# The first four tiles of x: loaded as rows and turned on TensorE in place of a transposing load, with new instruction orders

## The chip, the cores and the metric

The kernel runs on one core of one Trainium2 chip. The metric is the device time of one execution in microseconds (us); the number given for a kernel is the median of several runs. One execution of each kernel is also recorded by the hardware profiler. Its trace gives each instruction's start and length, counted from the start of the recorded span.

## The reference

The input x has 2048 rows of 448 columns, in bfloat16. The result mixes an attention block A and a token-mixing block B by a gate per row:

```python
x = A_x
g = _sigmoid((x * gate_w).sum(-1, keepdims=True))
a = _A_ref(x, A_wq, A_wk, A_wv, A_wo, A_beta)
b = _B_ref(x, B_w1, B_b1, B_w2, B_b2)
return g * a + (1 - g) * b
```

A projects x to q, k and v (16 heads of 28 columns) and works in four segments of 512 rows. In each segment it takes causal softmax attention within the segment, and adds, by a second gate per head, what a running memory of the earlier segments gives: the memory sums phi(k) v, with phi(t) = t + 1 above zero and exp(t) below. The heads are joined and multiplied by wo. B normalizes each row of x, multiplies over the rows with w1 (2048 by 1792), adds a bias, applies GELU, multiplies with w2 back to 2048 rows and adds a bias.

## The kernel before, in words

All work is written as small named operations, each with the data that it reads and writes. The class Sched turns them into instruction streams for five engines: TensorE (PE), ScalarE (ACT), VectorE (DVE), GpSimd (POOL) and SyncE (SP), of which SP issues most DMAs and ACT the first few. The order on each engine is not computed: the table ORDER spells it out, name by name, and some operations may stand on either of two engines, as the table says. Waits follow from the data. Each engine runs its list strictly in order, so an instruction that waits holds everything behind it.

x is used in two layouts. As rows (tile xh, 16 tiles of 128 rows) it feeds the normalization and B's first product. Turned (tile xT, the 448 columns cut into four overlapping chunks of 128 on the partitions, the rows along the free dimension) it feeds the projections. xT is filled in four groups of 512 rows, each by two transposing DMAs from device memory: dtx0_0 and dtx0_1 for the first group, dtx1, dtx2 and dtx3 for the later ones (transpose_x, line 546). The row tiles are loaded four at a time (load_x, line 532).

The program starts so. SP issues the two transposing loads of group 0, then parts of wk and wq, then the transposing loads of group 1, then the four row loads. ACT issues three parts of wv, the gate vector, the fourth part of wv, the last part of wk and two biases; then comes the one load of its activation table, which stands ahead of its first ACTIVATE. TensorE runs nine passes over a constant of ones (warm_up, line 660, operation warm), turns the gate vector (gtr), and then projects v for row tiles 0 to 3. A v tile is summed over four chunks of xT. Chunk 0 alone is the operation pra, chunk 1 prb, and the last two are one whole pass (prt) and a half of the array's rows in a step that two tiles share (lot0, lot2). The eight operations pra0 to pra3 and prb0 to prb3 thus come first, each one pass of 449 columns (448 and the gate's), and the lo steps follow. The first k products have names pra0_0 to pra0_2 and prk0_0 to prk0_2 and need wk copied into padded form by DVE (padk, padx; padq for wq). Two products that run side by side on half of the array's rows each are called half passes here; a pair of projections takes a lo step and six whole passes.

After that TensorE works through the projections, the scores (line 1015), the products of probabilities and v (line 1045), the two products of B (operations u and y) and the product with wo (operations lo and wo with the prefix w). ACT copies results out of PSUM (lines 773, 787, 835 for k and q, 857 for v), takes the exponentials of the scores (line 1024) and parts of GELU. DVE takes the row statistics (956), normalizes, copies (775 and others), transposes attention blocks, combines them, and makes the final mix of A and B (1251). POOL masks scores (1027) and adds attention and memory parts into output blocks (1082). The name of an operation ends with its tile or unit number, and a table word such as u3-9 means pass 9 of group 3; @ gives the PSUM bank.

Line 296 is the helper mm that issues the passes of most products, so the trace shows nearly all products under it.

Of the kernel before, what the change touches and what calls it, by code (L numbers as in the profile page):

```python
# [12 lines left out]
D = 448  # L13
# [5 lines left out]
NCT = 4  # L19
# [292 lines left out]
def pool_cost(n):  # L312
# [12 lines left out]
u1-15 u2-10*4 u3-5*2 u4-0@4 u3-7*2 sc1_1 u5-0@6*2 u2-14 u5-2*2 u2-15 u3-9*6 u5-4 u3-15 u4-1*5 u5-5*2 pv1@7 u4-6*2
sc1_2 u4-8 u5-7*5 u4-9*4 u5-12 pv0@5 u5-13 sc1_3 u4-13*3 u6-0@7*3 u7-0@5 u6-3 u5-14 u6-4*2 u5-15 u6-6 sc1_4 u6-7 u7-1
u6-8*4 u7-2*2 u6-12 u7-4*3 u6-13*3 sc2_0 u7-7*7 pv2@6 u7-14*2 sc2_1 mst0@4 u8-0@6*2 prq2_1@7 prq2_0@5 loq2_0 sc2_2
u8-2*4 prq2_2@4 u8-6*4 prq2_2h@7 loq2_2 mem1 u8-10*2 u9-0@4 u8-12 u9-1*8 u8-13*2 u11-0@5 sc2_3 u9-9*3 pv3@7 u9-12
u8-15 u9-13*2 u11-1 u9-15 u11-2*4 sc2_4 u10-0@7*3 u11-6*6 u13-0@4 u10-3 pv4@6 sc3_0 u10-4*12 u11-12 u13-1 sc3_1
u13-2*3 u11-13*2 u13-5*2 pv5@6 u11-15 prt9@7 u13-7*4 sc3_2 lot8@6 u13-11*2 u12-0@5*5 prt8 u13-13*3 u12-5 sc3_3  # L330
lot10@67 u12-6*3 prt11 u12-9*7 prt10 sc3_4 mst1@7 prk3_1@4 pv6@5 prk3_0@7 lok3_0 sc4_0 prq3_1@6 prq3_0@7 wo0@5 loq3_0
lw0@4 sc4_1 wo1 pv7@6 prk3_2@5 wo3@7 lok3_2@4 lw2@6 sc4_2 wo2 prx3_3 y0-0@5*5 mem2 y0-5*9 prq3_2h@6 prq3_2@4 loq3_2
sc4_3 y1-0@7*7 y2-0@4 y1-7 y2-1 sc4_4 y2-2*2 y1-8 y3-0@6*3 pv8@5 y2-4 y1-9 sc5_0 y2-5*2 y3-3*3 y1-10 y3-6*5 sc5_1
y3-11*3 y1-11*3 y2-7 wo4@5 sc5_2 lw4@7 wo5 y2-8 pv9@6 y2-9*2 sc5_3 y2-11*3 y5-0@5*7 sc5_4 lw6@64 y5-7 pv10@7 wo7
y5-8*2 sc6_0 y4-0@7 y5-10*4 wo6 y4-1*2 sc6_1 pv11@4 y4-3*3 y6-0@6*2 mst2@5 sc6_2 y4-6 y6-2*5 prt13@4 lot12@5 mem3
y6-7*5 y4-7*2 prt12 y4-9*2 y6-12*2 sc6_3 lot14@45 prt15 prt14 y4-11*3 sc6_4 pv12@5 y7-0@4*3 wo9@7 lw8@5 sc7_0 wo8
y7-3*7 sc7_1 y7-10*2 pv13@6 y7-12*2 y8-0@5*4 sc7_2 y8-4*2 y9-0@7*3 y8-6 wo10@6 y8-7 sc7_3 wo11@4 y8-8*4 y9-3 y8-12*2
y9-4 sc7_4 lw10 y9-5*5 pv14@5 y10-0@6*7 y9-10*2 pv15@4 y11-0@5 y10-7 y11-1*3 y10-8*2 y9-12*2 y11-4*5 y10-10*2 y11-9*3
lw12 lw14 y10-12 y11-12*2 y10-13 wo14 wo15 wo12 y12-0@4*2 wo13 y13-0@7*4 y15-0@5 y13-4*2 y14-0@6*2 y13-6*4 y12-2
y14-2*2 y13-10 y14-4 y12-3*2 y13-11 y12-5*3 y14-5 y15-1 y12-8*3 y14-6*3 y13-12*2 y12-11*3 y14-9*5 y15-2*12 y15-0#1@7  # L340
y15-1#1 y15-2#1 y15-3#1 y15-4#1 y15-5#1 y15-6#1 y15-7#1 y15-8#1 y15-9#1 y15-10#1 y15-11#1 y15-12#1 y15-13#1""",
    "ACT": """
ldwv0 ldgw ldwv1 ldwv2 ldwvb ldwkb ldb1 ldb2 cpv2 cpv0 gt0 gt2 cpv1 gt3 gt1 ek0_0 cpk0_1 cpk0_3 cpq0_3 ek0_1 cpv7 gt7
cpk1_3 cpq1_3 cpk1_2 cpv6 cpq0_2 gt6 cpq0_0 cpq0_2#1 cpq1_1 cpq1_2 cpq0_1 tb eq1_1 cpq1_2#1 exp0_0@2 cpk1_1 cpv5 cpv4
gt5 gt4 exp0_1@3 cpk2_2 cpk2_3 cpk2_1 exp0_2@4 cpk2_0 exp0_3@0 eq1_0 eq1_2 exp0_4@1 ek0_2 gsq0 exp1_0@5 gsq1 gvh1 gth0
exp1_1@6 gsq2 gth1 ek0_3 eq1_3 gsq3 gvh3 exp1_2@0 ek1_0 gth3 gth2 exp1_3@1 gsq4 gsq5 exp1_4@2 ek1_1 gth5 gth4 exp2_0@3
gsq6 gsq7 exp2_1@4 ek1_2 cpq2_1 exp2_2@5 ek1_3 cpq2_0 gth7 cpq2_2#1 gth6 eq2_2 eq2_0 exp2_3@6 gsq8 gsq9 eq2_1 gvh9
exp2_4@0 gth8 gth9 exp3_0@1 ek2_0 gsq10 ek2_1 gvh10 exp3_1@2 gsq11 gth10 exp3_2@3 cpv9 cpv8 gt8 gt9 gth11 exp3_3@4
cpv11 gsq13 gt11 gsq12 cpv10 exp3_4@0 gth12 gt10 cpk3_0 exp4_0@5 eq2_3 cpq3_1 cpq3_0 exp4_1@6 gth13 cpk3_2 exp4_2@7
cpk3_3 ag2 eq3_1 cpq3_3 ag3 ek2_2 exp4_3@1 ek2_3 exp4_4@2 eq3_0 exp5_0@0 eq3_2 exp5_1@3 exp5_2@4 exp5_3@5 ag5 exp5_4@6  # L350
eq3_3 exp6_0@1 ag6 exp6_1@2 exp6_2@7 cpv13 gt13 cpv12 gt12 exp6_3@0 gt15 gt14 exp6_4@3 exp7_0@4 ag9 exp7_1@5 exp7_2@6
exp7_3@1 exp7_4@2 ag11 ag15 ag14 ag12 ag13""",
# [39 lines left out]
def build_kernel(nc, X, WQ, WK, WV, WO, BETA, W1, B1, W2, B2, GW, OUT):  # L392
# [376 lines left out]
    def do_k(tc, hg, t0=0, n=512):  # L769
# [8 lines left out]
        if tc == 0:  # L778
            P["first"] = [((0, 1), [R_xT[0][0], R_wkp[0], R_wkp[3]])]
# [599 lines left out]
```

## Time and profile before

| what | before |
|---|---|
| time, median of 3 runs | 170.2 us (170.14 to 170.22) |
| the profiled execution | 170.1 us |
| its span | 168.3 us |
| PE busy | 164.0 us, 97% |
| DVE busy | 136.9 us, 81% |
| ACT busy | 130.4 us, 77% |
| POOL busy | 64.5 us, 38% |
| DMA | 25.44 MB, mean 151 GB/s |

Busy time is the time in which an engine has at least one instruction running. A row of the trace's timeline gives the start, the length, the engine and line, the operation, the tiles it writes and reads, shapes and a count of merged instructions; square brackets hold the idle time of the engine before the row, and what ended it. ACTq and SPq are the issuing of DMAs by ACT and SP. PEld is TensorE's loading of weights, which overlaps with PE. TensorE's passes are pipelined: a row's length includes the time until the last result is out, so neighbouring passes overlap in the table. A row that groups instructions gives the count, the busy time in us, the mean length of one in ns, and the idle time before them with its releasers.

### The profile page before, as it was taken

What the parts mean: (1) busy time and instruction counts of PE and PEld (TensorE: products, weight loads), DVE (VectorE), ACT (ScalarE), POOL (GpSimd) and SP (SyncE); (2) the same over time, 40 slices, a digit from 0 to 9 for tenths busy, and PEclk for the clock granted to TensorE, in tenths of its full rate; (3) what the DMA queues carried; (4) which work ended last, traced back from release to release, by engine and by line L of the source; (5) the groups of instructions that cost most, each with busy time, mean ns of one, the idle gap of its engine ahead of it and who ended that gap; (6) DMA issues with size and microseconds to landing.
All of it is one profiled execution on the core that took longest, in us unless ns stands there. A gap on an engine that the chain in (4) does not pass through costs nothing.

```text
span 168.3 us, 4931 instructions
## 1 busy us (share of the span) xinstructions
PE 164.0 (97%) x2017; PEld 77.6 (46%) x2017; DVE 136.9 (81%) x321; ACT 130.4 (77%) x164; POOL 64.5 (38%) x100
## 2 busy tenths in 40 slices
PE   8799999999999999999999999999999999999994
PEld 3234444444554544544453454444454444454553
DVE  0087999877989989999999999999999979695042
ACT  0359999999999997999999998988985798603200
POOL 5000245261442514142177356445838356541000
DMA  6999999886677955994338202328942129730302
GB/s 144 259 225 296 242 236 237 167 220 189 181 158 221 217 101 146 163 213 126 103 108 182 67 2 63 97 77 157 253 126 84 42 63 283 225 117 27 117 27 82
DMA packets 53974, 25.44 MB, mean 151 GB/s; under 512 B 18416, under 2 KB 53712, under 8 KB 53952
## 3 DMA queue, kind: packets, MB, share of 16 engines
q1 hardware_dynamic: 53160, 24.54, 59.2%
q10 hardware_dynamic: 792, 0.58, 1.6%
q8 instruction: 16, 0.26, 0.7%
q14 instruction: 6, 0.05, 0.1%
HBM read 18.82 MB, written 2.36 MB: 126 GB/s over the span
## 4 chain that ended last, share of the span: by engine, by line
PE 94%; DMA 3%; ACTq 1%; POOL 0%; issue 0%; DVE 0%; POOLq 0%
PE t L296 79%; PE t L1015 8%; PE t L1045 5%; DMA t<-in_A_wv_dram 3%; PE t L896 1%; PE t L1118 1%; ACTq L538 1%; ACTq L559 0%; DVE t L1251 0%; POOL t L557 0%; POOL t L633 0%; POOL t L600 0%; PE t L927 0%; POOL t L632 0%; POOL t L628 0%
## 5 line engine op out<-in xcount | busy, mean ns | idle before, releaser
L296 PE MATMUL t<-t 128*32 128x448 bf16 (+8 forms) x1252 | 140.5, 352 | 1.1 <-DMA t<-in_A_wv_dram 1.0
L296 PEld LDWEIGHTS t<-t 128*32 128x32 bf16 (+2 forms) x1252 | 63.0, 97 | 64.3 <-issue 14.2
L1024 ACT ACTIVATE t<-t 128x2048 bf16<-128x2048 f32 x40 | 75.2, 1879 | 6.8 <-PE t L1015 6.2
L1027 POOL TENSOR_SCALAR_AFFINE_SELECT t<-t 128x512 bf16<-128x512 bf16 x64 | 43.5, 691 | 42.5 <-ACT t L1024 39.6
L1082 POOL TENSOR_TENSOR t<-t 128x448 bf16<-128x448 f32 (+2 forms) x13 | 13.3, 1026 | 19.0 <-DVE t L1075 14.4
L1251 DVE SCALAR_TENSOR_TENSOR t<-t 128x448 bf16<-128x448 f32 (+2 forms) x17 | 10.7, 645 | 10.2 <-PE t L296 10.1
L1015 PE MATMUL t<-t 28*128 28x512 bf16 (+3 forms) x256 | 15.8, 301 | 0.0
L1059 DVE STREAM_TRANSPOSE t<-t 128x512 f32<-128x512 f32 x16 | 11.3, 706 | 2.9 <-PE t L1045 2.7
L965 POOL TENSOR_TENSOR t<-t 128x4 f32<-128x4 f32 x4 | 4.2, 1054 | 23.3 <-DVE t L963 21.6
L1157 ACT ACTIVATE t<-t 128x448 bf16<-128x448 f32 x10 | 7.0, 732 | 7.7 <-PE t L296 7.7
L1045 PE MATMUL t<-t 128*32 128x512 bf16 (+3 forms) x256 | 11.5, 299 | 0.0
L1101 DVE STREAM_TRANSPOSE t<-t 128x512 bf16<-128x512 bf16 x16 | 10.9, 690 | 0.0
L1015 PEld LDWEIGHTS t<-t 28*128 28x128 bf16 x256 | 4.4, 92 | 14.0 <-ACT t L1024 7.7
L956 DVE BATCH_NORM_STATS2 t<-t 128x6 f32<-128x448 bf16 x16 | 9.3, 610 | 1.1 <-DMA t<-in_A_x_dram 1.1
L857 ACT ACTIVATE t<-t 128x448 bf16<-128x448 f32 x13 | 6.8, 546 | 4.2 <-PE t L296 4.2
L1220 DVE SCALAR_TENSOR_TENSOR t<-t 128x448 f32<-128x448 f32 x14 | 9.2, 664 | 0.5 <-ACT t L1215 0.4
L1045 PEld LDWEIGHTS t<-t 128*32 128x32 bf16 x256 | 6.7, 97 | 5.3 <-issue 0.4
L1212 ACT ACTIVATE t<-t 128x448 f32<-128x448 f32 x14 | 8.8, 638 | 0.1
L818 ACT ACTIVATE t<-t 128x512 bf16<-128x512 bf16 x12 | 7.6, 635 | 1.4 <-DVE t L775 1.4
L847 DVE SCALAR_TENSOR_TENSOR t<-t 128x512 bf16<-128x512 bf16 x12 | 8.5, 712 | 0.1
L1075 DVE SCALAR_TENSOR_TENSOR t<-t 128x448 f32<-128x448 f32 x12 | 8.4, 698 | 0.0
L1225 DVE SCALAR_TENSOR_TENSOR t<-t 128x448 bf16<-128x448 f32 x14 | 8.4, 614 | 0.0
(76 smaller groups left out, 129.3 us busy)
## 6 DMA issues: line engine op xcount, KB each, us to landing
t<-in_B_w_dram SPq DMA_DIRECT2D x52, 256.0 KB, 3.4
t<-in_A_x_dram SPq DMA_DIRECT2D x4, 448.0 KB, 4.8
out_dram<-t SPq DMA_DIRECT2D x15, 112.0 KB, 1.9
t<-in_B_w_dram SPq DMA_DIRECT2D x8, 128.0 KB, 2.4
t<-in_A_wv_dram ACTq DMA_DIRECT2D x4, 112.0 KB, 4.1
t<-in_A_wq_dram SPq DMA_DIRECT2D x1, 336.0 KB, 5.1
spare_heads<-t SPq DMA_DIRECT2D x8, 32.0 KB
spare_heads<-t SPq DMA_DIRECT2D x16, 16.0 KB
```

The lines of the kernel that those rows point to most:

```text
L296: last = e.matmul(out[q], w[:, q], x, skip_group_check=True, **kw)
L956: op("DVE", lambda e: e.bn_stats(st6[:, t, :], xh[:, t, :]), reads=[R_x[t]], writes=[R_st6[t]], name=f"bns{t}", cost=512, prio=P_PROJ - 10 ...
L1015: last = e.matmul(bank(hl)[:, c0 : c0 + w], kT[r, hg, s * 512 + j * 128 : s * 512 + j * 128 + 128], qT[r, hg, s * 512 + 128 * j : s * 512 ...
L1024: exps.append(op("ACT", lambda e: e.activation(pslot(g), ps[:, 0:4, :], ACT.Exp, scale=SCALE), reads=R_bank[0:4], writes=[g.res], take=g, ...
L1027: op("POOL", lambda e, c0=c0: e.affine_select(pslot(g)[:, :, c0 : c0 + 128], pslot(g)[:, :, c0 : c0 + 128], pattern=[[0, 4], [1, 128]], co ...
L1045: last = e.matmul(bank(cb)[32 * ((hl + hg) % 4) : 32 * ((hl + hg) % 4) + 32, 128 * j : 512], vaug[:, 4 * s + j, 32 * h : 32 * h + 32], psl ...
L1059: dv(lambda e: e.transpose(tt[:, ia, :], bank(cb)[:, 0:512]), [bres(cb)], [R_tt[ia]], "ta", 630, use=(cb,))
L1082: return e.tensor_tensor(dst, part(n3[0]), part(n3[1]), op=ALU.add)
L1101: dv(lambda e: e.transpose(oT[:, hg, s * 512 : s * 512 + 512], o), [R_ob[hg]] + ([R_obx] if hg else []), qres(hg, s), "ot", 635)
L1212: op("ACT", lambda e: e.activation(gg[:, q, :], bank(b)[:, 0:D], ACT.Square, bias=b1s[:, ft : ft + 1], scale=math.sqrt(GC)), **buse(b), re ...
L1220: op("DVE", lambda e: e.scalar_tensor_tensor(gg[:, q, :], gg[:, q, :], 1.0, vh[:, q, :], op0=ALU.add, op1=ALU.mult), reads=[R_gg[q], R_vh[ ...
L1251: op("DVE", lambda e: e.scalar_tensor_tensor(outst[:, p, c0:c1], bank(b)[:, 0 : c1 - c0], omg[:, T : T + 1], ag(T)[:, c0:c1], op0=ALU.mult ...
```

## The change

The transposing loads of group 0 go (dtx0_0, dtx0_1), and so does the load of row tiles 0 to 3 in one piece. In their place stand four row loads of one tile each: tiles 0 and 2 on SP, tiles 1 and 3 on ACT. They are each queue's first loads of x; on ACT the gate vector's load stands between the two. Of wv, parts 0 and 2 move to SP and parts 1 and 3 stay on ACT. The last part of wk moves from ACT to SP.

Each of the four tiles is turned by TensorE: four passes (one for each chunk) have the tile's 128 columns as weights and the identity as the moving operand, so the bank receives the turned chunks side by side. One copy for each tile (cx0 to cx3) brings a bank's 512 columns as bf16 into xT. By the table cx0 and cx2 are DVE's, cx1 and cx3 ACT's. The passes of ones go from nine to six. What reads group 0 of xT now waits for the copies of the tiles that it needs, by xres.

```diff
-    transpose_x(0)
+    for t, eng in enumerate(("SP", "ACT", "SP", "ACT")):
+        load_x(eng, t, 1)
     load_w(lambda: wvx, WV, R_wv, "wv", None, "ACT")
-    load_w(wk_nat, WK, R_wk, "wk", P_wk, "ACT")
+    load_w(wk_nat, WK, R_wk, "wk", P_wk, "SP")
...
     transpose_x(1)
-    load_x("SP", 0, 4)
...
-            op("ACT" if len(r) == 4 else "SP", lambda e, c0=c0, c1=c1: e.dma_start(
+            op("ACT" if len(r) == 4 and k == 1 else "SP", lambda e, c0=c0, c1=c1: e.dma_start(
...
-    warm_up(9, "warm", -1)
+    def turn_x():
+        for t in range(4):
+
+            def fn(e, t=t):
+                for c in range(NCT):
+                    last = e.matmul(bank(t)[:, 128 * c : 128 * c + 128], xh[:, t, C0[c] : C0[c] + 128], ident[:, :],
+                                    start=True, stop=True, skip_group_check=True)
+                return last
+
+            op("PE", fn, reads=[R_x[t], R_ident], writes=[R_bank[t]], name=f"xt{t}", mode="f",
+               cost=pe_cost(128, 128, 128, 128), prio=-1)
+
+            def ends(t=t):
+                return xT[:, :, 128 * t : 128 * t + 128], bank(t).rearrange("p (c t) -> p c t", c=NCT)
+
+            op("ACT", lambda e, ends=ends: e.activation(*ends(), ACT.Copy), reads=[R_bank[t]], writes=[R_xT[0][t]],
+               name=f"cx{t}", cost=act_cost(512), prio=-1,
+               alt=("DVE", lambda e, ends=ends: e.tensor_copy(*ends()), dve_cost(512)))
+
+    warm_up(6, "warm", -1)
     warm_up(1, "warm2", P_PROJ + 0.01, 3500.0)
+    turn_x()
...
+    def xres(tc, cs=range(NCT), tiles=range(4)):
+        return [R_xT[0][k] for k in tiles] if tc == 0 else [R_xT[tc][k] for k in sorted({c // 3 for c in cs})]
```

The table ORDER is new for all five engines. Its first line for TensorE, before and after:

```diff
-warm gtr@4 warm2 pra0@5 pra1@6 pra2@7 pra3@4 prb3 prb2 prb0 prb1 lot2 lot0 prt1 prt3 prt2 prt0 pra0_1 pra0_2 pra0_0
+warm xt0 xt1 gtr@4 warm2 xt2 xt3 pra1@5 pra0@6 prb0 prb1 pra2@7 pra3@4 prb2 prb3 lot0 lot2 prt3 prt0 prt2 pra0_1
```

The new table differs in three kinds of things. Operations stand in another order: within a group of u or y passes the single passes too, and the DMAs on SP. Operations that may stand on either of two engines change the engine: of the steps that write an output block (o, ox, oy) twelve stand on DVE where two did, of the v copies four where three did, of the gate mixes (ag) nine where six did. And seven pairs of products (the words that begin with dt, dk, dq and dw) are written as fourteen half passes each in place of a lo step and six whole passes, as are single passes of groups u12 and y0 (the words u12x, u12y, y0x, y0y); the functions that do so, halves and both, were there before.

More of the change, by code (lines that the diff above doesn't have):

```diff
@@ L325 @@
[L325 to L339, printed above, removed]
@@ L346 @@
[L346 to L350, printed above, removed]
@@ L499, in build_kernel @@
     R_x = R("x", NT)
-    R_xT = [R(f"xT{t}_", 2) for t in range(4)]
+    R_xT = [R(f"xT{t}_", 4 if t == 0 else 2) for t in range(4)]
+    def xres(tc, cs=range(NCT), tiles=range(4)):
+        return [R_xT[0][k] for k in tiles] if tc == 0 else [R_xT[tc][k] for k in sorted({c // 3 for c in cs})]
     R_phk = [R(f"phk{s}_", NHG) for s in range(3)]
@@ L778, in do_k @@
         if tc == 0:
-            P["first"] = [((0, 1), [R_xT[0][0], R_wkp[0], R_wkp[3]])]
+            P["first"] = [((0, 1), xres(0, (0, 1)) + [R_wkp[0], R_wkp[3]])]
         return P
```

135 lines of the change are left out of this document (85 added, 50 removed).

## Prediction

> **What bounds the kernel now.** I read the page first (busy shares, the chain that ended last), then the start of the chain in order of time, then timelines of TensorE, the ACT queue, DVE and the SP queue over the first 13 us, and last a table of busy time by stretch.
>
> ```profile
> span 168.3 us, 4931 instructions
> PE 164.0 (97%) x2017; PEld 77.6 (46%) x2017; DVE 136.9 (81%) x321; ACT 130.4 (77%) x164; POOL 64.5 (38%) x100
> PE 94%; DMA 3%; ACTq 1%; POOL 0%; issue 0%; DVE 0%; POOLq 0%
> ```
>
> TensorE is the bound: 164.0 of 168.3 us, and 94% of the chain. What it does not fill lies at the two ends. The chain in order of time starts so:
>
> ```profile
> 2.34 0.56 ACTq L538
> 2.93 4.36 DMA t<-in_A_wv_dram
> 7.43 2.78 PE t L296 x14
> ```
>
> The last 128 rows of wv are issued at 2.93 and land at 7.29; TensorE goes on at 7.43. TensorE's timeline over that stretch (start, length, line, shape, count, idle before):
>
> ```profile
> 0.82 3.38 PE L664 MATMUL t<-const-bfloat16-1.0 128*128 128x512 bf16 x9 [0.82 <-PEq L1364]
> 4.59 0.92 PE L296 MATMUL t<-t 128*128 128x449 bf16 x4
> 5.91 0.93 PE L296 MATMUL t<-t 128*128 128x449 bf16 x4 [0.40 <-DMA t<-in_A_wv_dram]
> 7.43 2.78 PE L296 MATMUL t<-t 64*128 64x449 bf16 x14 [0.59 <-DMA t<-in_A_wv_dram]
> 10.14 0.11 PEld L296 LDWEIGHTS t<-t 64*128 64x128 bf16 x2
> 10.54 0.10 PEld L296 LDWEIGHTS t<-t 64*128 64x128 bf16 x2 [0.30 <-DVE t L675]
> ```
>
> Nine passes of ones, eight first passes of the v projection in two groups of four, and from 7.43 on work without gaps but for one hold, on DVE's padding of the weights. The pace of passes is read further on:
>
> ```profile
> 30.12 2.44 PE L296 MATMUL t<-t 128*128 128x448 bf16 x12
> 35.59 0.39 PE L1015 MATMUL t<-t 28*128 28x512 bf16 x4
> 35.91 0.36 PE L296 MATMUL t<-t 128*128 128x448 bf16 x1
> ```
>
> Twelve 448-column passes in 2.44, the last with its 0.35 of latency, give 0.19 each, so 0.22 for 512 columns. Four scores passes run side by side and should take 0.22; the next shape starts after 0.32, so a change of tile shape costs 0.10. The half passes at 10.14 should thus be followed after 0.22 and are followed after 0.40: a hold of 0.18. A run without it that ends when this one ends would begin its half-pass step ("lo") at 7.43 + 0.18 = 7.61. I take 7.61 as the before side of the start.
>
> From there TensorE is full to the end:
>
> ```profile
> 40.00:140.00 100.00, 100.00 (x1509) 47.95 (x1502) 93.41 (x198) 92.20 (x106) 46.07 (x64) 1.00 0.53 130
> 140.00:160.00 20.00, 20.00 (x241) 9.98 (x240) 12.11 (x21) 7.94 (x8) 6.51 (x8) 1.00 0.49 146
> ```
>
> The columns are the stretch, then PE, PEld, DVE, ACT and POOL busy, granted clock, DMA. PE has 100.00 of 100.00, but DVE has 93.41 and ACT 92.20: both are close behind. So the time can move in three ways only: the moment at which gapless work begins, the TensorE work itself, and a new wait because DVE or ACT is late.
>
> **The change part by part. The start.** What must be there for the first v pass is now the copy of a turned tile, and the order puts tile 1 first, whose copy stands on ACT. The ACT instructions of before, at the program's start:
>
> ```order
> L538 DMA t<-in_A_wv_dram 128x448
> L559 DMA t<-in_gate_w_dram 6x128
> L538 DMA t<-in_A_wv_dram 128x448 x2
> L542 DMA t<-in_A_wv_dram 128x448
> L542 DMA t<-in_A_wk_dram 128x448
> L568 DMA t<-in_B_b_dram 14x128
> L570 DMA t<-in_B_b_dram 16x128
> L857 ACT_TABLE_LOAD
> L857 ACTIVATE t<-t 128x16x28 x2
> ```
>
> and now (L703 is the copy cx1, then cx3):
>
> ```order
> L551 DMA t<-in_A_x_dram 128x448
> L578 DMA t<-in_gate_w_dram 6x128
> L551 DMA t<-in_A_x_dram 128x448
> L556 DMA t<-in_A_wv_dram 128x448
> L560 DMA t<-in_A_wv_dram 128x448
> L586 DMA t<-in_B_b1_dram 14x128
> L588 DMA t<-in_B_b2_dram 16x128
> L703 ACT_TABLE_LOAD
> L703 ACTIVATE t<-t 128x4x128 x2
> ```
>
> Seven issues in place of eight, and then the table load, which used to stand in front of work that TensorE delivered late and now stands in front of cx1, for which TensorE waits. The ACT queue of before in time:
>
> ```profile
> 0.78 0.38 ACTq L538 DMA_DIRECT2D t<-in_A_wv_dram  x1
> 1.20 0.73 ACTq L559 DMA_DIRECT2D t<-in_gate_w_dram  x1
> 1.96 0.94 ACTq L538 DMA_DIRECT2D t<-in_A_wv_dram  x2
> 2.93 0.61 ACTq L542 DMA_DIRECT2D t<-in_A_wv_dram  x1
> 3.57 0.64 ACTq L542 DMA_DIRECT2D t<-in_A_wk_dram  x1
> 4.71 0.37 ACTq L570 DMA_DIRECT2D t<-in_B_b_dram  x1
> 5.12 1.28 ACT L857 ACT_TABLE_LOAD   x1 [5.12 <-issue]
> 8.70 0.98 ACT L857 ACTIVATE t<-t 128x448 bf16<-128x448 f32 x2 [2.30 <-PE t L296]
> ```
>
> The last issue ends at 4.71 + 0.37 = 5.08. The five 112 KB issues take 0.38, 0.47, 0.47, 0.61 and 0.64, 0.51 in the mean; one fewer, with its gap of 0.03, ends the last at 4.54. Table load 0.03 + 1.28 to 5.85 (before, it was over at 6.40 and ACT then sat idle for 2.30, so it cost nothing). The copy of 512 columns from PSUM to bf16:
>
> ```profile
> L773 ACT ACTIVATE t<-t 128x512 bf16<-128x512 f32 x8 | 4.8, 604 | 0.3 <-PE t L296 0.3
> L775 DVE CAST t<-t 128x512 bf16<-128x512 f32 x4 | 2.7, 673 | 0.3 <-PE t L296 0.2
> ```
>
> 0.60 on ACT brings cx1 to 6.45. A signal costs 0.05 (the padding that TensorE waited for ended at 10.49, the weight load began at 10.54):
>
> ```profile
> 10.19 0.30 DVE L675 COPY t<-t 128x224 bf16<-128x224 bf16 x2 [0.46 <-DMA t<-in_A_wq_dram]
> ```
>
> So the first v pass starts at 6.50. Eight of them at 0.19 end at 8.02, and with the change of shape the lo step starts at 8.12, against 7.61: **+0.51**. The second copy on ACT, cx3, ends about 0.6 after cx1, at 7.05; the pass that reads it is the sixth, at 7.45, and is not held.
>
> What else the start needs lies under this. TensorE's order at the program's start was (L664 passes of ones, L879 and L880 the gate vector's turn, L296 the helper of most products)
>
> ```order
> L664 MATMUL t<-const-bfloat16-1.0 128x512 x9
> L879 MATMUL t<-t 128x3
> L880 MATMUL t<-t 128x1
> L664 MATMUL t<-const-bfloat16-1.0 128x512
> L296 MATMUL t<-t 128x449 x16
> ```
>
> and is (L682 the passes of ones, L693 the identity passes)
>
> ```order
> L682 MATMUL t<-const-bfloat16-1.0 128x512 x6
> L693 MATMUL t<-t 128x128 x8
> L919 MATMUL t<-t 128x3
> L920 MATMUL t<-t 128x1
> L682 MATMUL t<-const-bfloat16-1.0 128x512
> L693 MATMUL t<-t 128x128 x8
> L296 MATMUL t<-t 128x449 x15
> ```
>
> Three passes of ones go, sixteen identity passes come, all ahead of the first v pass.
>
> ```profile
> L296 PE MATMUL t<-t 128*128 128x128 bf16 x14 | 0.9, 219 | 0.0
> t<-in_A_wv_dram ACTq DMA_DIRECT2D x4, 112.0 KB, 4.1
> ```
>
> A 128-column pass costs (0.9 - 0.22) / 13 = 0.05, so sixteen cost 0.9, at most twice that at the slow pace of the first passes; without the cover of ACT's table load they would be a delay of that size. A 112 KB row load landed 4.1 after its issue in the median, beside transposing loads. By that bound tile 0 or 1 lands at 4.9, tile 3 (issued near 2.0) at 6.1, the last part of wv (issued near 3.0) at 7.1: each before it is needed (xt1 by 5.85, cx3 by 6.45, lo by 8.12). On DVE, one normalization statistic, cx0 (0.67), gw and cx2 come before the paddings; even from 4.9 on that is 0.6 + 0.67 + 0.2 + 0.67, so gw at 6.4 and cx2 at 7.0; gw is needed at 6.50 and tile 2 at 7.26. On SP two transposing loads go, four row loads come ahead of wk and one more part of wk behind it, and the old four-tile load of x goes; wq and the next transposing pair move slightly earlier, so no later queue entry is pushed back. DVE's padding hold at 10.54 should not return, as k passes come 0.5 later.
>
> **The TensorE work.** A projection pair is two half passes side by side plus six whole ones, seven slots; written as half passes it is fourteen in seven slots. The same holds for the second matrix products, so slots are equal. Shape changes, counted in both programs' order, are 113 against 112: **+0.10**.
>
> **The tail.** Before, the program ended on TensorE with
>
> ```order
> L296 MATMUL t<-t 128x448 x20
> L296 MATMUL t<-t 128x320
> L296 MATMUL t<-t 128x448 x16
> L296 MATMUL t<-t 128x320 x12
> L296 MATMUL t<-t 128x128 x14
> ```
>
> and now with
>
> ```order
> L296 MATMUL t<-t 128x448 x20
> L296 MATMUL t<-t 128x128
> L296 MATMUL t<-t 128x448 x3
> L296 MATMUL t<-t 128x128 x2
> L296 MATMUL t<-t 128x448 x5
> L296 MATMUL t<-t 128x128 x11
> ```
>
> A whole tile now closes eleven short passes before the end, 0.6 us, where the long run of short and 320-column passes used to give DVE time.
>
> ```profile
> 163.57 0.68 DVE L1251 SCALAR_TENSOR_TENSOR t<-t 128x448 bf16<-128x448 f32 x1 [0.24 <-PE t L296]
> 165.98 0.35 DVE L1251 SCALAR_TENSOR_TENSOR t<-t 128x128 bf16<-128x128 f32 x1 [0.23 <-PE t L296]
> ```
>
> That tile's mix (0.68) starts 0.16 after the last whole pass has streamed and ends 0.84 after; the last short pass is ready at 0.55 + 0.22 = 0.77. So the last mix is held by 0.1, at least 0, at most about 0.3 if the tile before is late too: **+0.1**.
>
> **The stretch between.** Work moves to DVE: twelve steps that write an output block stand there in place of two, four v copies in place of three, nine gate mixes in place of six, besides cx0 and cx2.
>
> ```profile
> L1082 POOL TENSOR_TENSOR t<-t 128x448 bf16<-128x448 f32 x8 | 9.5, 1182 | 14.1 <-DVE t L1075 11.0 <-DVE t L1077 2.0 <-DVE t L982 1.2
> L1082 DVE TENSOR_TENSOR t<-t 128x448 bf16<-128x448 f32 x1 | 0.6, 625 | 0.0
> L859 DVE CAST t<-t 128x448 bf16<-128x448 f32 x3 | 1.8, 623 | 0.3 <-PE t L296 0.3
> ```
>
> Between 40 and 140 these are six such steps (two of 0.62, four smaller of about 0.5: 3.2) and two v copies (1.2): 4.4 us into 100 - 93.4 = 6.6 us of idle. The rest falls after 140, where DVE has 12.11 of 20. The bounds for TensorE are a gain of 0.2 (POOL's 1.18 becomes DVE's 0.62 in the chain to an output block, though no TensorE idle hangs on it today) and a loss of about 1.2 (below); nearest is the PE column, full at a DVE load of 93%, so I take **+0.2**.
>
> **The sum.** 0.51 + 0.10 + 0.1 + 0.2 = 0.9. The profiled execution took 170.1 (span 168.3, 1.8 around it), so 171.0; the median of the runs is 170.2, 0.1 above it, so **171.1** as a median. About 0.2%, 0.34 us, is what a measurement of this kernel can tell from no change. The sum's own range is 170.6 to 171.7: its start may be 0.2 off either way (issues of 0.47 or 0.61 in place of 0.51 and a copy of 0.55 to 0.70), the stretch -0.2 to +0.5.
>
> **The rivals.** *Faster: the ACT queue is quick.* The long issues (0.61, 0.64) stood beside SP's own row loads and transposes; the shortest took 0.37. The lo step is the end of the last issue E plus 0.03 + 1.28 + 0.60 + 0.05 + 1.52 + 0.10 = E + 3.58, so the start gains from E below 4.03. With seven issues of 0.375 E is 3.58, lo is at 7.16, -0.45; with the shape change and nothing lost later, 170.2 - 0.35 = 169.85. For it: transposes leave the rings. Against it: SP now issues nine row loads in the same stretch, the gate's load took 0.73. It decides from E = 3.6 down; chance 0.13.
>
> *No change:* E near 4.1 to 4.3 and no loss in the tail or between: 170.2 to 170.5. Chance 0.16.
>
> *DVE becomes the bound between 40 and 140.* If only half of the 6.6 us idle can be used, because it lies where TensorE has not delivered, 4.4 - 3.3 = 1.1 us of evictions come late, and in-order TensorE waits: 171.1 - 0.2 + 1.2 = 172.1. For it: 93%; against: POOL's share falls, and its masks no longer queue behind additions. Chance 0.14.
>
> *ACT is not ready right after the table load.* The trace shows its length and no more: the next ACT instruction began 2.30 after its end, but waited for TensorE. So readiness is bounded by 0 and 2.30; half of it gives 172.2. Chance 0.06. [...]
>
> *TensorE's clock is down when the v passes begin.*
>
> ```profile
> L664 PE MATMUL t<-const-bfloat16-1.0 128*128 128x512 bf16 x10 | 3.6, 532 | 0.8 <-PEq L1364 0.8
> L296 PE MATMUL t<-t 128*128 128x512 bf16 x57 | 14.2, 380 | 0.0
> ```
>
> The first 512-column passes take 532 ns in the mean, later ones 380; the nine took 3.38, where nine at 0.22 would take 2.1. Now only six passes of ones stand at the start and TensorE is nearly empty from about 4.9 to 6.5, where its longest hole was 0.59. If it starts again slowly and needs the same 3.3 us to speed up, half of that is lost: 171.1 + 1.6 = 172.7. Chance 0.07. [...]
>
> **How the numbers follow.** The forecast has 0.44, faster 0.13, no change 0.16, DVE 0.14, ACT 0.06, clock 0.07. Slower by over 0.2% is 0.44 + 0.14 + 0.06 + 0.07 = 0.71; same 0.16; faster 0.13. The range from 169.7 to 172.5 holds all but the clock case, the upper parts of the DVE and ACT cases and the fastest part of the faster one.
>
> **What would show it.** Right: in the new profile the table load starts at 4.5 to 4.7, cx1 is named as releaser of the first v pass, that pass starts at 6.4 to 6.7, the lo step near 8.1, and TensorE is then full to the end. Wrong: a first v pass before 6.0, released by wv or gw; passes at the slow pace after 6.5; TensorE idle behind DVE between 40 and 140; or a wait on a gather of heads, whose DMAs stand in a new order on SP and whose wait I price at nothing because none is seen now.

## The result and the profile after

After the change the kernel takes 175.0 us, median of 4 runs (174.67 to 175.31), against 170.2 us before (4 runs beside them, 170.14 to 170.84). The ratio is 1.027, with a 95% interval of 1.024 to 1.031: slower by 4.7 us, and 2.5 us beyond the top of the range that was forecast. The profiled execution of after took 174.67 us, its span 172.5. Of all the runs below one, 176.75 us of the kernel with three masks moved, lies over 1.5% above the fastest of its kernel and is left out there as slow.

The page of after, its first rows and the shares of the chain that ended last:

```profile
span 172.5 us, 5173 instructions
PE 164.9 (96%) x2130; PEld 77.9 (45%) x2135; DVE 153.7 (89%) x339; ACT 128.3 (74%) x160; POOL 61.2 (35%) x90
PE 77%; DVE 16%; DMA 2%; ACT 1%; POOL 1%; issue 1%; POOLq 0%; ACTq 0%
```

DVE had 0% of the chain before; now it has 16%. Its busy time went from 136.9 to 153.7 us, 16.8 more, where the prediction had counted 4.4 us of added work between 40 and 140 us and gave no figure for the rest. The table of busy time by stretch (columns as in the prediction: stretch, then PE, PEld, DVE, ACT, POOL) shows where TensorE stands still, first before, then after:

```profile
57.00:95.00 38.00, 38.00 (x636) 18.66 (x632) 36.19 (x78) 36.64 (x50) 16.45 (x23) 1.00 0.63 144
147.00:158.00 11.00, 11.00 (x140) 5.65 (x133) 6.82 (x13) 2.57 (x4) 2.59 (x3) 1.00 0.34 104
```

```profile
57.00:95.00 38.00, 36.17 (x604) 17.37 (x603) 37.45 (x75) 35.17 (x49) 17.59 (x20) 1.00 0.51 118
147.00:158.00 11.00, 9.80 (x174) 5.22 (x175) 10.10 (x16) 3.97 (x3) 6.17 (x8) 1.00 0.37 108
```

TensorE loses 1.83 us in the first stretch and 1.20 in the second, 3.0 of the 4.2 us by which the span grew; PE's busy time grew by 0.9: 0.29 of it lies in the first 8 us, where the identity passes are, and the tables don't take the rest apart. The waits of TensorE in after (us in total, times, longest), without the one before its first pass, one of 0.2 and four short holes, 0.7 in sum, that the profile puts down to no releaser:

```profile
PE t L1085 <- POOL t L1067: 1.2, 1, 1.2
PE t L693 <- DMA t<-in_A_x_dram: 0.8, 1, 0.8
PE t L296 <- ACT t L898: 0.6, 1, 0.6
PE t L1055 <- DVE t L1166: 0.5, 1, 0.5
PE t L1158 <- DVE t L954: 0.3, 1, 0.3
```

The line numbers of these later parts are up by 38 to 40 against before: L1085 are the products of probabilities and v, L1067 the causal masks on POOL, L1055 the scores, L693 the identity passes.

Now the start, from the timelines of ACT and of PE in after:

```profile
4.08 1.28 ACT L703 ACT_TABLE_LOAD   x1 [4.08 <-issue]
5.37 0.60 ACT L703 ACTIVATE t<-t 128x512 bf16<-128x512 f32 x1
```

```profile
5.91 0.40 PE L693 MATMUL t<-t 128*128 128x128 bf16 x4 [0.81 <-DMA t<-in_A_x_dram]
6.15 3.12 PE L296 MATMUL t<-t 128*128 128x449 bf16 x16
```

ACT's issues were over by 4.05 and cx1 by 5.97, but the turn of tile 3 stands ahead of the first v pass in TensorE's order, and that tile was there only shortly before 5.91, so the pass came at 6.15. Taken pass by pass, the lo step came at 7.82, and the first scores at 20.76, as before (20.73): of the start's delay nothing was left by then. So the loss lies behind it.

The lengths of single steps are what has changed there. The masks as a group, before and after:

```profile
L1027 POOL TENSOR_SCALAR_AFFINE_SELECT t<-t 128x512 bf16<-128x512 bf16 x64 | 43.5, 691 | 42.5 <-ACT t L1024 39.6
L1067 POOL TENSOR_SCALAR_AFFINE_SELECT t<-t 128x512 bf16<-128x512 bf16 x64 | 49.0, 785 | 54.7 <-ACT t L1064 53.8
```

A mask that meets no two-input DVE step, and a two-input DVE step that starts while no mask runs (one starts in its last 0.16 us), both of before, and then a piece of after, DVE and POOL in order of time:

```profile
138.57 0.64 POOL L1027 TENSOR_SCALAR_AFFINE_SELECT t<-t 128x512 bf16<-128x512 bf16 x1 [0.54 <-ACT t L1024]
```

```profile
67.87 0.68 DVE L1089 SCALAR_TENSOR_TENSOR t<-t 128x448 bf16<-128x448 f32 x1
```

```profile
59.69 0.69 DVE L860 SCALAR_TENSOR_TENSOR t<-t 128x512 bf16<-128x512 bf16 x1
...
59.84 1.04 POOL L1067 TENSOR_SCALAR_AFFINE_SELECT t<-t 128x512 bf16<-128x512 bf16 x1 [9.20 <-ACT t L1064]
...
60.30 1.05 DVE L1129 SCALAR_TENSOR_TENSOR t<-t 128x448 bf16<-128x448 f32 x1
```

```profile
60.83 1.01 POOL L1067 TENSOR_SCALAR_AFFINE_SELECT t<-t 128x512 bf16<-128x512 bf16 x1
```

The mask at 59.84 begins inside DVE's step of 59.69, which ends at 60.38, and ends 0.50 later, at 60.88. The DVE step at 60.30 begins inside that mask and ends 0.47 after it, at 61.35; the next mask begins inside that step and ends 0.49 after it. Each ends about half a us after the other and is 0.37 to 0.40 longer than by itself. I call a DVE step long when it takes over 0.2 us more than the lower quartile of its kind (its name without the numbers) in the two traces. In before 9 of 321 are long, in after 33 of 339. Three or four of the long steps of every kernel here are so only by their shape, a larger block than most of their kind has: three of the 9, four of the 33. That leaves 6 and 29. Each of these began while a POOL step was running, in after 28 times a mask and once an addition; of the 29, 20 have two inputs and 9 have one. The final mix (L1291), one of whose two inputs is a PSUM bank, began inside a mask with over 0.4 us of it still to run three times in after (fin3, fin7, fin8) and took 0.67 to 0.68 us, no longer than elsewhere.

### The profile page after: what moved, and what is told of

It is laid out like the page before. It is cut to its first block, busy times and chain, and to the rows that moved or that the text cites. A ratio compares the mean times of both kernels' runs of the same rounds, so it can differ in the third digit from the quotient of the medians.

```text
span 172.5 us, 5173 instructions
## 1 busy us (share of the span) xinstructions
PE 164.9 (96%) x2130; PEld 77.9 (45%) x2135; DVE 153.7 (89%) x339; ACT 128.3 (74%) x160; POOL 61.2 (35%) x90
## 4 chain that ended last, share of the span: by engine, by line
PE 77%; DVE 16%; DMA 2%; ACT 1%; POOL 1%; issue 1%; POOLq 0%; ACTq 0%
PE t L296 64%; PE t L1055 6%; PE t L1085 5%; DMA t<-in_A_x_dram 2%; DVE t L1265 2%; DVE t L860 2%; DVE t L885 2%; DVE t L1129 1%; DVE t L1260 1%; DVE t L1166 1%; ACT t L1064 1%; PE t L936 1%; DVE t L1099 1%; DVE t L1141 1%; DVE t L1258 1%
## 5 line engine op out<-in xcount | busy, mean ns | idle before, releaser
L296 PE MATMUL t<-t 128*32 128x448 bf16 (+11 forms) x1352 | 140.2, 350 | 1.2 <-issue 0.7
L1067 POOL TENSOR_SCALAR_AFFINE_SELECT t<-t 128x512 bf16<-128x512 bf16 x64 | 49.0, 785 | 54.7 <-ACT t L1064 53.8
L1055 PE MATMUL t<-t 28*128 28x512 bf16 (+3 forms) x256 | 15.8, 301 | 0.5 <-DVE t L1166 0.5
L1197 ACT ACTIVATE t<-t 128x448 bf16<-128x448 f32 x7 | 4.8, 721 | 14.4 <-PE t L296 14.4
L1291 DVE SCALAR_TENSOR_TENSOR t<-t 128x448 bf16<-128x448 f32 (+2 forms) x17 | 10.8, 643 | 2.6 <-PE t L296 2.3
L1085 PE MATMUL t<-t 128*32 128x512 bf16 (+3 forms) x256 | 11.5, 300 | 1.4 <-POOL t L1067 1.2
L1055 PEld LDWEIGHTS t<-t 28*128 28x128 bf16 x256 | 4.5, 92 | 14.0 <-ACT t L1064 6.2
L895 ACT ACTIVATE t<-t 128x448 bf16<-128x448 f32 x12 | 6.4, 543 | 4.8 <-PE t L296 4.8
L1201 DVE TENSOR_SCALAR t<-t 128x448 bf16<-128x448 f32 x9 | 6.7, 739 | 3.6 <-PE t L296 3.6
L1085 PEld LDWEIGHTS t<-t 128*32 128x32 bf16 x256 | 6.5, 96 | 7.2 <-POOL t L1067 1.8
L1265 DVE SCALAR_TENSOR_TENSOR t<-t 128x448 bf16<-128x448 f32 x14 | 9.6, 689 | 0.1
L1122 POOL TENSOR_TENSOR t<-t 128x448 bf16<-128x448 f32 x4 | 4.9, 1233 | 13.6 <-DVE t L1117 9.2
L885 DVE SCALAR_TENSOR_TENSOR t<-t 128x512 bf16<-128x512 bf16 x12 | 9.4, 788 | 0.1
L1252 ACT ACTIVATE t<-t 128x448 f32<-128x448 f32 x14 | 8.8, 631 | 0.8 <-PE t L296 0.5
L1260 DVE SCALAR_TENSOR_TENSOR t<-t 128x448 f32<-128x448 f32 x14 | 9.0, 642 | 0.1
L1263 ACT ACTIVATE t<-t 128x448 f32<-128x448 f32 x14 | 8.1, 578 | 1.3 <-DVE t L1260 1.3
```

Source lines behind the costliest of these rows:

```text
L296: last = e.matmul(out[q], w[:, q], x, skip_group_check=True, **kw)
L885: op("DVE", lambda e: e.scalar_tensor_tensor(ph, qs, 0.0, ph, op0=ALU.max, op1=ALU.add), reads=qres(hg, tc) + [R_phq[hg][tc]], writes=[R_p ...
L1055: last = e.matmul(bank(hl)[:, c0 : c0 + w], kT[r, hg, s * 512 + j * 128 : s * 512 + j * 128 + 128], qT[r, hg, s * 512 + 128 * j : s * 512 ...
L1067: op("POOL", lambda e, c0=c0: e.affine_select(pslot(g)[:, :, c0 : c0 + 128], pslot(g)[:, :, c0 : c0 + 128], pattern=[[0, 4], [1, 128]], co ...
L1085: last = e.matmul(bank(cb)[32 * ((hl + hg) % 4) : 32 * ((hl + hg) % 4) + 32, 128 * j : 512], vaug[:, 4 * s + j, 32 * h : 32 * h + 32], psl ...
L1260: op("DVE", lambda e: e.scalar_tensor_tensor(gg[:, q, :], gg[:, q, :], 1.0, vh[:, q, :], op0=ALU.add, op1=ALU.mult), reads=[R_gg[q], R_vh[ ...
```

## The experiments

The theory that came out of the trace was first "DVE": DVE has more to do than it can finish. Its rivals were "start" (the new way to xT costs) and "GpSimd" (the masks are late, as the first row of the waits says).

**The start alone, and the orders alone.** The first run is after with before's orders behind the start; its TensorE order (here against before) and the second run's (against after), at the program's start:

```diff
-warm gtr@4 warm2 pra0@5 pra1@6 pra2@7 pra3@4 prb3 prb2 prb0 prb1 lot2 lot0 prt1 prt3
+warm xt0 xt1 gtr@4 warm2 xt2 xt3 pra1@6 pra0@5 prb0 prb1 pra2@7 pra3@4 prb2 prb3 lot0 lot2 prt1 prt3
```

```diff
-warm xt0 xt1 gtr@4 warm2 xt2 xt3 pra1@5 pra0@6 prb0 prb1 pra2@7 pra3@4 prb2 prb3 lot0 lot2 prt3
+warm gtr@4 warm2 pra1@5 pra0@6 prb0 prb1 pra2@7 pra3@4 prb2 prb3 lot0 lot2 prt3
```

> The kernel after with its new start alone: the four row loads, the identity passes and their copies stand where the change puts them, and from there on every engine has the order of before, output steps on GpSimd included. Theory 'DVE' (the new orders put more work on VectorE than it can finish, and TensorE waits for it): the start costs only what the profile of after shows of it, the first left-over pass 0.2 us later, so 170.2 to 170.8 us. Rival 'start' (the new way to xT is what costs): 173 us or more.

> The kernel before with its old start (DMA transposes of the first x tiles), and the orders of after from there on; the norm statistics of the first four tiles stand a little later on VectorE, since the old start brings those rows later. Theory 'DVE': nearly the whole loss is here, 174.0 to 175.0 us, with TensorE behind VectorE between 57 and 95 us and a wait at the attention product of unit 14. Rival 'start': 170 to 171 us.

The start alone took 170.24 us against 170.26 for before, a ratio of 0.999 (0.998 to 1.001): it costs nothing that can be measured. The orders alone took 178.0 (1.046, 1.039 to 1.053), more than after itself and 3.0 above the top of what was expected. So "start" falls. The second run is no clean half: its first scores came at 22.92 instead of 20.76, because the old start brings wk and the row tiles at other times than the new orders want them (its chain up to 30 us goes through a load of wk and then through DVE).

**The ten output steps back on POOL.** The steps are taken out of DVE's list and put into POOL's at about the time at which they ran, oy12, ox12, o14 and o15 behind the last mask:

```diff
-eps7 gvh11 b2g1 oy4 garg11 ta5
+eps7 gvh11 b2g1 garg11 ta5
...
-mask3_0_0 mask3_1_1 mask3_2_2
+mask3_0_0 oy4 mask3_1_1 mask3_2_2
...
-mask7_4_1 mask7_4_3
+mask7_4_1 mask7_4_3 oy12 ox12 o14 o15
```

> The kernel after with the ten output steps that went from GpSimd to VectorE (ox0, oy4, ox4, ox8, o9, o10, oy12, ox12, o14, o15) back on GpSimd; nothing else differs. Theory 'DVE': 6.3 us of VectorE's work go, the stretch 57 to 95 us loses little since only two or three of the ten stand in it, the wait at unit 14 goes: 172.5 to 173.9 us. Rival 'GpSimd' (the masks on GpSimd are what TensorE waits for): 1 us or more slower than after, since GpSimd has 8.8 us more ahead of its masks.

It took 177.34 us (1.041, 1.037 to 1.044), 2.4 more than after: the number that "GpSimd" named, not mine. The chain shows two parts. Up to 80 us nearly nothing changed; the product of unit 5, the end of the long stretch behind DVE, in this run and in after:

```profile
80.05 0.71 PE t L1085 x16
```

```profile
80.14 0.73 PE t L1085 x16
```

Of the ten steps at most one stands ahead of it in that stretch (oy4, from 79.99 in after), so they can't be what fills it. And at the end TensorE waited 2.2 us for DVE and 0.7 for a gather, since I had put the last four steps behind the masks (the chain goes from the last mask through two additions on POOL, 154.32 to 155.56, to DVE). So the run says that the ten steps aren't the cause between 57 and 80 us, and nothing more.

**The wait at unit 14.** Two edits of DVE's order at the end:

```diff
-om13 oa13 oy12 o13 ox12 eps14 fin9 ot13 ta14
+om13 oa13 fin9 oy12 o13 ox12 eps14 ot13 ta14
```

```diff
-om13 oa13 oy12 o13 ox12 eps14 fin9 ot13 ta14 omg3 rec14 ta15 ot12
+om13 oa13 fin9 oy12 ox12 eps14 ta14 omg3 rec14 o13 ta15 ot13 ot12
```

> The kernel after with one step moved on VectorE: the final step of tile 9 (fin9) ahead of the output steps oy12, o13, ox12 instead of behind them. Theory 'DVE': the wait of 1.2 us of the attention product of unit 14, which the waits of the profile put down to the last mask, is for the PSUM bank that fin9 empties, so it goes and the time falls by 0.7 to 1.3 us, to 173.6 to 174.3. Rival 'GpSimd' (it waits for the mask, as the profile names it): no change, 174.8 to 175.1 us.

> The kernel after with VectorE's order changed at the end: fin9 ahead of oy12, o13 and ox12 (as in the run with that step alone, which left a wait of 0.9 us one product later, for the transpose of unit 14 that stood behind these steps), and o13 and ot13 behind that transpose. Theory 'DVE late': both waits go, 173.4 to 174.0 us. Rival 'GpSimd late' (the products wait for the last masks): 174.3 us or more.

The first took 174.43 us (1.024, 1.021 to 1.026), the second 173.76 (1.020, 1.019 to 1.022). The waits of the first name another releaser for the products:

```profile
PE t L1085 <- DVE t L1020: 0.9, 1, 0.9
```

and in the second the products of units 14 and 15 run without a wait:

```profile
152.44 0.71 PE L1085 MATMUL t<-t 128*32 128x512 bf16 x16
152.98 1.31 PE L296 MATMUL t<-t 128*32 128x448 bf16 x24
154.11 0.72 PE L1085 MATMUL t<-t 128*32 128x512 bf16 x16
```

The order of the masks is the same in both, so "GpSimd" falls here, though the profile of after names the mask: in the first run none of TensorE's waits is put down to POOL, where after has one of 1.2, and in the second the product of unit 14 begins at 152.44 instead of 153.68. The one step that moved ahead in the first is fin9, on DVE, so I take it that the product had waited for the PSUM bank that fin9 empties. The first run's time lies between the two ranges that were expected. By its time alone the first run can't be told from after (the intervals touch); the second can.

**Short masks.** By now the 33 long steps were counted, and the theory became "port": a DVE step with two inputs in SBUF and a POOL step that reads SBUF hold each other up. (The 33 include the four that are larger blocks and nine with one input; "nearly all" with two inputs, in the expectation, says too much.) Rival: "amount", DVE simply has more steps. The edit, in after and in before:

```diff
-e.affine_select(pslot(g)[:, :, c0 : c0 + 128], pslot(g)[:, :, c0 : c0 + 128],
-                pattern=[[0, 4], [1, 128]], ...)
+e.affine_select(pslot(g)[:, :, c0 : c0 + 16], pslot(g)[:, :, c0 : c0 + 16],
+                pattern=[[0, 4], [1, 16]], ...)
```

> The kernel after with each causal mask on GpSimd cut from 128 to 16 columns, in the same place of the same orders (most of the masking is left out). Theory 'port': 33 of VectorE's steps in after are some 0.4 us longer than the same steps elsewhere, nearly all of them steps with two SBUF inputs that meet a running mask; with masks that short most of these meetings go, VectorE's busy time falls from 153.7 to about 142 to 146 us, and TensorE's waits behind VectorE go with it: 171.3 to 172.7 us. Rival 'amount' (VectorE simply has more steps to do): the waits stay, 174.2 to 175 us, with VectorE busy over 150 us.

> The control: the kernel before with the same cut of the masks to 16 columns. In before 9 steps of VectorE are long and TensorE waits for none of them, so theory 'port' and rival 'amount' both expect no change here, 170.0 to 170.4 us; VectorE's busy time falls by about 3 us, to 133 to 135. If it gets faster by 1 us or more, shorter masks help for another reason, and the run of after with short masks says nothing on the port.

After with short masks took 170.84 us (1.0036, 1.0023 to 1.0049), 4.1 less than after and 0.5 below the range of "port"; before with short masks 170.19 (0.999, 0.998 to 1.000). The masks now take 0.33 us, no DVE step is long but the four larger blocks, and the page has

```profile
PE 164.0 (97%) x2130; PEld 78.1 (46%) x2135; DVE 143.2 (85%) x339; ACT 128.1 (76%) x160; POOL 31.8 (19%) x90
```

DVE is busy 10.5 us less for 29 long steps fewer, 0.36 each. A group of two-input steps (L885) and one of one-input steps (L882), in after and here:

```profile
L885 DVE SCALAR_TENSOR_TENSOR t<-t 128x512 bf16<-128x512 bf16 x12 | 9.4, 788 | 0.1
L882 DVE TENSOR_SCALAR t<-t 128x512 bf16<-128x512 bf16 x12 | 5.0, 415 | 0.1
```

```profile
L885 DVE SCALAR_TENSOR_TENSOR t<-t 128x512 bf16<-128x512 bf16 x12 | 8.1, 683 | 0.1
L882 DVE TENSOR_SCALAR t<-t 128x512 bf16<-128x512 bf16 x12 | 3.3, 279 | 0.1
```

**Fills that read nothing.** Short masks also leave POOL free sooner (it is busy for 31.8 us in place of 61.2). So the mask's place was taken by a write of the same block:

```diff
-e.affine_select(pslot(g)[:, :, c0 : c0 + 128], pslot(g)[:, :, c0 : c0 + 128], ...)
+e.memset(pslot(g)[:, :, c0 : c0 + 128], 1.0)
```

> The kernel after with each causal mask on GpSimd replaced by a fill of the same 128x512 block with ones, in the same place of the same orders: it writes the block and reads nothing, and should take 0.5 to 0.6 us, near the mask's 0.63 (the masking is left out). It tells what about the short masks helped. Theory 'port' (a GpSimd step that reads SBUF and a VectorE step with two SBUF inputs hold each other up): the meetings of two-input steps cost nothing any more, 170.6 to 171.8 us. Rival 'GpSimd late' (the attention products wait for GpSimd to be through with its masks, so shorter masks helped by being shorter): nearly as slow as after, 173.5 us or more.

It took 170.87 us (1.005, 1.002 to 1.008), with POOL nearly as long at each block as a mask is by itself (0.53 us against 0.64):

```profile
L1067 POOL MEMSET t<- 128x512 bf16 x64 | 32.7, 533 | 67.3 <-ACT t L1064 66.6
```

Nine steps are long, the four larger blocks and five with one input, none with two; the two-input group stays at its short length, while the one-input group (TENSOR_SCALAR from SBUF to SBUF, 283 ns in the mean in before) is still lengthened by the fills:

```profile
L885 DVE SCALAR_TENSOR_TENSOR t<-t 128x512 bf16<-128x512 bf16 x12 | 8.1, 685 | 0.1
L882 DVE TENSOR_SCALAR t<-t 128x512 bf16<-128x512 bf16 x12 | 4.4, 369 | 0.1
```

So for two-input steps it isn't POOL's being busy that costs: they take 685 ns beside fills and 788 beside masks. A fill differs from a mask in that it reads nothing, though also in the operation, and no run takes these two apart; nor does a row show what holds a step up. One-input steps are lengthened by either, less by fills than by masks (369 ns against 415). And a step that came second wasn't held back whole: in after it ended behind the other by 0.47 to 0.50 us, less than its own 0.64 to 0.68.

**Other orders, the same steps.** Three masks moved on POOL, and seven steps moved on DVE (mk1_1, oa2, ot2, phq2_1, eps6, ot8, oy12; each is shown in the middle of its new place):

```diff
-mask1_2_2#1 mask2_1_1 mask1_3_0 mask1_4_1 mask1_4_3 mask2_0_0
+mask1_2_2#1 mask1_3_0 mask1_4_1 mask1_4_3 mask2_1_1 mask2_0_0
```

```diff
+omg1 mk1_0 mk1_1 phk1_0 msta0
+tm4 tm7 oa2 tm6 tm5
+mk1_2 phk1_3 ot2 phq2_0 gelu8
+ta5 ot3 phq2_1 garg10 phk2_1
+phk2_0 cpv10 eps6 ot4 oa5
+rec9 oa9 ot8 ag5 mk2_2
+oa12 rec13 oy12 ag11 ag10
```

> The kernel after with three masks moved on GpSimd: mask1_3_0, mask1_4_1 and mask1_4_3 ahead of mask2_1_1, for which they wait until 59.8 us though their exponentials are long done (GpSimd is busy 0.8 of the 10 us from 50, and 6.6 of the 10 from 60). Theory 'port': fewer masks run while VectorE is behind, oa1, mstc0, oa2 and garg7 lose some of their 0.4 us each, and the waits between 63 and 80 us shrink by 0.5 to 1.5 us in sum: 173.4 to 174.5 us. Rival 'amount': no change, 174.7 to 175.2 us.

> The kernel after with seven steps of VectorE moved by 2 to 7 places in VectorE's own order (ot2, oa2, oy12, phq2_1, mk1_1, ot8, eps6), and nothing else: the same steps on the same engines, and the orders of the four other engines as in after. The places were chosen so that fewer two-input steps meet a mask while TensorE is about to wait. Theory 'port': most of the 4 us come back, 171.0 to 172.3 us. Rival 'amount' (VectorE has too much to do, wherever it stands): 174.0 us or more.

The three masks gave 174.15 us (1.021, 1.019 to 1.024), 0.8 less than after but with an interval that touches after's: 31 steps are long, mstc0 and garg7 no longer. The seven moves gave 173.17 (1.017, 1.014 to 1.019), 1.8 less than after and outside its interval, yet 0.9 more than the top of what "port" expected; "amount", which named 174.0 or more, is missed too. 29 steps are long in it; its moves took some long steps off the path and made others long, and the stretches still have waits:

```profile
57.00:95.00 38.00, 36.91 (x615) 17.88 (x611) 37.40 (x77) 36.27 (x50) 15.76 (x20) 1.00 0.54 120
147.00:158.00 11.00, 10.59 (x211) 5.95 (x211) 10.06 (x19) 3.75 (x2) 5.64 (x8) 1.00 0.42 120
```

**The converse in before.** Three DVE steps moved, and, in another kernel, the ten output steps put on DVE, with fourteen other DVE steps up to seven places off to make room for them (two pieces shown):

```diff
-garg12 oa5 garg13 ot4 ta6 cpk3_1
+garg12 ta6 oa5 garg13 ot4 cpk3_1
...
-mk1_3 eps4 phk1_3 oa2 ta3 mq2_0
+mk1_3 ta3 eps4 phk1_3 oa2 mq2_0
...
-ag8 om12 ta13 ot12 rec13 fin7 om13
+ag8 fin7 om12 ta13 ot12 rec13 om13
```

```diff
+ot3 oa4 oy4 gelu11 ox4 gelu10
...
+ag8 om12 ox12 oy12 ta13 ot12
```

> The converse: the kernel before with three steps of VectorE moved three to four places ahead (ta6, ta3, fin7), nothing else. The steps that they change places with then meet masks while TensorE is about to wait. Theory 'port': 1.5 to 4 us slower than before, 171.7 to 174.2 us, with TensorE waiting behind VectorE. Rival 'amount': no change, 170.0 to 170.5 us.

> The kernel before with the ten output steps that the change moves from GpSimd to VectorE moved there (ox0, oy4, ox4, ox8, o9, o10, oy12, ox12, o14, o15), at places in VectorE's order at which few two-input steps meet a mask; fourteen other steps of VectorE stand up to seven places off for that. All else is before. Theory 'port': VectorE's 5 to 6 us more of work fit into its idle time, 170.0 to 171.2 us. Rival 'amount': 172 us or more.

The three moves took 172.91 us (1.015, 1.013 to 1.016), 2.6 more than before, with 14 long steps and waits of TensorE in the stretches where before has none:

```profile
PE t L1045 <- DVE t L1251: 0.8, 1, 0.8
PE t L296 <- DVE t L1059: 0.5, 1, 0.5
PE t L1045 <- POOL t L1027: 0.5, 1, 0.5
```

The ten steps on DVE took 170.11 (0.9989, 0.9980 to 0.9998): no loss, though DVE has ten steps more. 11 steps are long, and the chain is TensorE's:

```profile
PE 98%; DVE 0%; issue 0%
```

So the added steps, which I first took for the cause, are harmless in before, in an order chosen for them, and three moved steps do harm without any added amount.

**DVE ordered anew in after.** Three kernels ask whether the rest comes back with whole masks and every step on its engine. An example of each edit, from the third:

```diff
-oa2 ot1 garg7 tm4 tm7 tm6 tm5 gelu7 mk1_3 mq2_0 garg8 ta3
+gvh7 garg7 cpq2_1 ot1 omg1 gelu6 tm4 tm6 tm7 tm5 gelu7 mq2_0 mk1_3 oa2 garg8 ta3
```

> The kernel after with VectorE's steps in a new order throughout, chosen so that two-input steps meet few masks and TensorE waits for none; each step on its engine, masks whole, the orders of the four other engines as in after. Theory 'port': about 18 long steps in place of 33, no wait of TensorE above 0.3 us behind VectorE, 170.9 to 171.8 us. Rival 'amount': what the seven moves gave is all there is, 172.8 to 173.5 us.

> As the run with VectorE's order alone, but GpSimd's steps are ordered anew too (the masks by up to eight places); TensorE, ScalarE and the load queue as in after. Theory 'port': some 12 long steps, 170.7 to 171.3 us; if GpSimd's order of masks is part of the cause, 0.3 us or more better than the run with VectorE's order alone. Rival 'amount': 172.8 us or more.

> The kernel after with VectorE's order changed from 40 us on alone, no step by more than 13 places, so that two-input steps meet few masks and those of the last tiles keep their turn; each step on its engine, masks whole, the orders of the four other engines as in after. Theory 'port': about 20 long steps in place of 33, no wait of TensorE above 0.3 us behind VectorE after 50 us, 170.8 to 171.9 us. Rival 'amount': no better than the seven moves, 172.8 us or more.

The first two missed: 174.43 us (1.024, 1.019 to 1.029) and 175.28 (1.029, 1.024 to 1.033), no better than after; the first lies above the ranges of both theories, the second in that of "amount". The first has 22 long steps, and its last pass on TensorE ends 2.8 us earlier than in after (167.2 against 170.0), but the span is the same: four final steps of the last tiles are left to DVE behind it, until 169.2, and the outputs of these tiles are issued only from then on. The second waits, among others, for a gather of heads that its order brought late, at 41.47 to 44.58 in its chain. The third took 172.56 (1.014, 1.009 to 1.019), 2.4 less than after and between the ranges of "port" and "amount". Its profiled execution, the fastest of its four, took 171.61, and shows TensorE full where after has its holes, with 18 long steps:

```profile
57.00:95.00 38.00, 38.00 (x643) 18.58 (x639) 37.15 (x82) 37.17 (x51) 15.22 (x20) 1.00 0.54 123
147.00:158.00 11.00, 11.00 (x230) 6.19 (x231) 10.06 (x21) 3.32 (x2) 4.45 (x7) 1.00 0.44 124
```

So "amount" falls for these stretches: in this execution the same work fits. But its four runs lie between 171.61 and 173.47, 1.9 apart where after's are 0.6 apart, and why is not settled; nor is whether an order of after's steps reaches 170.8. No kernel here is clearly faster than before: the best, the ten steps on DVE, is within 0.2% of it.

## Why the prediction was wrong

**The bound and the start: right in kind, too dear.** TensorE was the bound, and ACT's queue, table load and copy followed each other as worked out. But the issues were quicker: the last ended at 4.05, not 4.54, so cx1 ended at 5.97, not 6.45. The first v pass came at 6.15 and the lo step 0.2 late instead of 0.51, released by the turn of tile 3. The prediction had that tile land at 6.1, in time for its copy, and did not count that its turn stands ahead of the first v pass. With before's orders behind it the start costs -0.1 us (interval -0.4 to +0.1), that is, nothing. The rivals on the start fall with it: ACT began 0.01 us after the table load's end, and the v passes ran at the full pace, 16 in 3.12 us, 0.19 each, behind a hole of 0.81. The passes of ones are slow in after too, 620 ns in the mean, but the granted clock is 1.00 over these first 4 us in both kernels, so neither trace shows a lower clock at the start.

**Shape change and tail: small, as said.** What after costs without the long steps is 0.6 us (1.0036 of before, short masks) or 0.9 (fills). The sum for start, shape change and tail was 0.7. That the two agree is in part luck, as the start was 0.51 of it and costs nothing by itself; no run here takes the other terms apart.

**The stretch between: the step that failed.** It set the moved steps, 4.4 us between 40 and 140, against 6.6 us of DVE's idle time, and took +0.2, with 1.2 as the worst. The runs give 4.1 in its place, what short masks take off after's time. The sign that had been named for it came: TensorE is idle for 1.85 of the 100 us between 40 and 140, and of its waits there 1.0 is put down to DVE and 0.6 to an ACT step (L898) that the chain reaches through DVE. A further 1.20 is lost between 147 and 158, where the prediction had counted on DVE's room after 140. Two things in the step were wrong. It priced each step at its length in before, as if the length went with the step. In fact 6.7 us of the added time on DVE belong to steps that stand on DVE in both kernels and only got longer. (Its list of moved steps, like that of the change, leaves out the k and q copies, of which six came to DVE and four left it.) The amount by itself would have fitted: with short masks, and all of after's steps on DVE, DVE is busy for 91.0 of those 100 us, where it was 93.4 in before. And it gave POOL's lighter load as a reason against trouble. What counts is not how much POOL does but which DVE step runs when a mask does: POOL was busy 61 us instead of 64, and held up 29 DVE steps instead of 6. A sign of it was there before: the masks' mean of 691 ns against 640 for one by itself. New orders on both engines change who meets whom, and that has to be counted as a term.

**The rivals.** "DVE becomes the bound" named the place, and the profile of after does show DVE in the chain from 58 to 80 us. Its mechanism, too little usable idle time for added steps, is refuted: ten added steps cost nothing in before, and the waits of after behind DVE go when masks are short. It also missed the size, 1.2 for 4.1. That the new orders cost by themselves, with no step added, was not among the rivals.

## What to carry to other kernels

When a change reorders VectorE or GpSimd, list the VectorE steps with two SBUF inputs first, those with one behind them (9 of the 29 here), and the GpSimd steps that read SBUF (here the masks, and once an addition), and look for pairs that would now run at once: here such a meeting made the step that came second about 0.4 us longer, and 23 more long VectorE steps, where TensorE was about to wait, cost a TensorE-bound kernel 4 us. In a profile, compare the mean length of the same group before and after; a busy time that grows by more than the steps added is a sign of this: here a held-up step stood in the trace as a longer one (1.05 us at 60.30 in after, with no wait before it), and DVE was busy for 10.5 us more than with short masks. And a releaser named for a wait on several things is not always the cause: here a mask was named for 1.2 us, and with fin9 alone moved that wait was gone. Moving the suspected step, with all else alike, settles it.

## What the runs showed that was not expected

Replacing two transposing loads by row loads and passes on TensorE moved the time by nothing (0.999), though it removes the old start's waits on wv: another wait, for the row tiles, stands in their place. A fill of 128x512 that only writes left two-input steps as short as short masks do (685 ns against 683), while one-input steps still lengthened (369 ns in the mean against 279 with short masks and 283 in before). And three DVE steps moved by three or four places cost 2.6 us: they made five steps more long (14 for 9), so 0.5 us of time for each, above the 0.37 by which a step got longer.
